# Output projection of attention as a phase of its own, with one level of Strassen, O through DRAM

## The chip, the cores and the metric

One core of a Trainium2 chip. The metric is the device time in microseconds (us) of one execution, the median of several runs. A core has five engines that matter here: PE (TensorE, matmul; its weight loads are listed as PEld), DVE (VectorE), ACT (ScalarE), POOL (GpSimd) and SP (SyncE), which issues nearly all of this kernel's transfers (DMA) from one queue, in order.

## The reference

```python
def _A_ref(x, k_cache, v_cache, wq, wo):
    ...
    Hq, Dh = 32, 128
    W = min(4096, max(256, Sk // 4))
    ...
    scores = jnp.einsum("bhqd,bhkd->bhqk", q, k) * (Dh ** -0.5)
    p = _softmax(scores, axis=-1)
    o = jnp.einsum("bhqk,bhkd->bhqd", p, v)
    return (lambda x, *d: x.transpose(*d))(o, 0, 2, 1, 3).reshape(B, Sq, Hq * Dh) @ wo
...
mod = (_silu(c) @ w_mod).reshape(c.shape[0], 6, 1, -1)
sa, ca, ga, sb, cb, gb = (mod[:, 0], mod[:, 1], mod[:, 2], mod[:, 3], mod[:, 4], mod[:, 5])
h = _layernorm(x, axis=-1) * (1 + ca) + sa
x = x + ga * _A_ref(h, A_k_cache, A_v_cache, A_wq, A_wo)
h = _layernorm(x, axis=-1) * (1 + cb) + sb
x = x + gb * _B_ref(h, B_w_gate, B_w_up, B_w_down)
```

x has 2048 rows of 576 channels; 32 query heads share 16 heads of keys and values, of which the last 512 rows count. `_B_ref` is a gated FFN with 4608 hidden channels. Everything is float32; a product is made as three matmuls of float32r operands that are split into a high and a low part (hi x lo, lo x hi, hi x hi).

## The kernel before

**Attention** works in blocks: one head and 512 rows of x, 4 tiles of 128 rows each. There are 128 blocks in an order `seq`, in two halves of 64 (rows 0 to 1023, then 1024 to 2047), and N = 512 steps n, one for each tile. A step of the main loop issues, for different blocks at once: a quarter of the query projection two blocks ahead (`qproj`, PSUM tile qp), the scores of tile n + 2 (`scores`, st), the transposes of tile n (`transp`, st again), the exponential of tile n + 2 (`expo`), one of four parts of P times V of the block before (`pv`, ot), and both halves of one tile of the output projection of the block before that (`wo_acc`, wo). `wo_acc` has three matmuls for each half of 288 columns; DVE then takes the result from PSUM, divides it by the sum of its softmax row (rs) and adds it to x, which stays in SBUF as four tiles xs[0] to xs[3]. Before that, ACT and DVE split O (tile ov) into its parts, and the rows of wo are loaded for each head, multiplied by the gate on POOL, and split on ACT and POOL (`load_o`, `scale_o`, `split_o`).

**Weights of the FFN** are prepared beside attention. The FFN itself uses one level of Strassen, and its operands' sums are formed and split by 135 jobs: 72 for gate and up ("ab"), after each eight of them one for the channels left over ("tail"), and 54 for down. A job is loaded at step n (`bg_load`), summed on POOL at n + 3, split on ACT and POOL at n + 6 and n + 7, and stored to DRAM at n + 8 and n + 9 (`bg_store`, tensors wsc and dsc). A new job starts every 3 steps. A job's room is used again three jobs later. An ab job has 3 loads and 3 stores, a tail job 4 loads and 24 stores, a down job 4 loads and mostly 3 stores. The rooms lie in those halves of x that are not in use: xs[2] and xs[3] in the first half, xs[0] and xs[1] in the second; around the change of halves no job runs.

**The order.** From step 8 on, the kernel's main instructions on each engine are held in the program's order (`keep_order`, `pin`); those that are not pinned may be moved by the scheduler of the tile framework. All these transfers leave from SP's one queue. A DMA that has to wait for a semaphore holds those behind it.

**FFN.** 72 rounds of seven products (PSUM tiles a, b, c) with sums of down projections between them (PSUM tile w, matmuls of 288 columns). Its operands come from scr (normalised x, in seven Strassen sums, formed in the second half of attention from xs[0] and xs[1]), wsc and dsc; the first of them are loaded while attention ends.

Of the kernel before, what the change touches and what calls it, by code (L numbers as in the profile page):

```python
# [13 lines left out]
OP = mybir.AluOpType  # L14
# [30 lines left out]
def adaln_block_kernel(ctx: ExitStack, tc: tile.TileContext, x, k_cache, v_cache, wq, wo, w_gate, w_up, w_down,  # L45
# [25 lines left out]
    actx = ExitStack()  # L71
    wp = actx.enter_context(tc.tile_pool(name="wp", bufs=1))
# [6 lines left out]
    def ps_sc():  # L79
        return psum("st", 3, [P, BLK])  # L80

    def ps_pt():
        return psum("st", 3, [P, BLK])
# [7 lines left out]
    def ps_wide():  # L91
        return psum("wo", 2, [P, BLK])
# [194 lines left out]
    at = actx.enter_context(tc.tile_pool(name="at", bufs=1))  # L287
# [8 lines left out]
    sbc = at.tile([P, NC + 1, P], F32, tag="ov", name="sbc", bufs=2)  # L296
    extra = at.tile([P, 4 * P], F32, tag="extra", name="extra")
    scale, shift, gate = mod_rows("scale", wp), mod_rows("shift", wp), mod_rows("gate", wp)
# [59 lines left out]
    load_mod(2, range(NC + 1))  # L358
# [6 lines left out]
    p2 = [ps_wo(), ps_wo()]  # L365
# [12 lines left out]
    p2 = [ps_wo(), ps_wo()]  # L378
# [20 lines left out]
    gate2 = [ps_wo(), ps_wo()]  # L399

    def gate_mm(ks):
        mod_mm(2, ks, gate2)
        if NC in ks:
            for j in range(2):
                nc.scalar.activation(gate[:, j * D2 : (j + 1) * D2], gate2[j], AF.Copy)

    def chunks1(ks):
        if 0 in ks:
            new_hT(1)
        for k in ks:  # L410
            p = ps_wide()
            for t in range(TPB):
                ln_channels(1, t, k, p)
            ln_shifted(1, k, p)


    RA, SA, RB, SB, KR, KS, VR, VS = {}, {}, {}, {}, {}, {}, {}, {}
    wm = {}
    QT, SUM, RS, PP, PT, OT, OP_, QP = {}, {}, {}, {}, {}, {}, {}, {}
# [74 lines left out]
    def expo(n):  # L494
# [21 lines left out]
    def pv(b, k):  # L516
# [7 lines left out]
        if k == KT - 1:  # L524
            o = at.tile([P, 2, BLK], F32R, tag="ov", name="ov", bufs=2)
            keep_order(nc.scalar.activation(o[:, 0, :], OP_[b], AF.Copy))
            nc.vector.tensor_sub(o[:, 1, :], OP_[b], f32(o[:, 0, :]))
            OT[b] = o
            del OP_[b], PT[b]

    def wo_acc(b, i, j):
        half, hd, blk = blk_of(b)
        cols = slice(i * P, (i + 1) * P)
# [33 lines left out]
    inst, inst_of = [], []  # L567
    for b, (half, hd, blk) in enumerate(seq):
        hh = half * H + hd
        for i in (len(inst) - 1, len(inst) - 2):  # L570
            if i >= 0 and inst[i][0] == hh:
                break
        else:
            i = len(inst)
            inst.append([hh, b, b])
        inst[i][2] = b
        inst_of.append(i)

    def load_o(i):
        RB[i] = load_b(wo, (inst[i][0] % H) * DH)  # L580

    def scale_o(hh):
        pin(nc.gpsimd.tensor_mul(RB[hh], RB[hh], gate))

    def split_o(hh):
        SB[hh] = split_b_hi(RB[hh])

    def split_o_lo(hh):
        split_b_lo(RB.pop(hh), SB[hh])

# [23 lines left out]
    at_n(-3, gate_mm, (0,))  # L614
# [8 lines left out]
    at_n(0, gate_mm, (1,))  # L623
    at_n(2, gate_mm, (2,))
    at_n(3, gate_mm, (3, 4))
# [10 lines left out]

    def o_first(i):
        return TPB * (inst[i][1] + 2)

    def o_free(i):  # L640
        return TPB * (inst[i][2] + 3)
# [12 lines left out]
    for hh in range(len(inst)):  # L654
        n = max(o_first(hh) - 7, o_free(hh - 2) if hh > 1 else 5)
        assert n < o_first(hh)
        at_n(n - 5, load_o, hh)
        at_n(max(n - 2, 4), scale_o, hh)
        at_n(n, split_o, hh)
        at_n(min(n + 1, o_first(hh) - 1), split_o_lo, hh)  # L660
    for b in range(2, NB):
        at_n(N // 2 - 34 + b, load_x, b)
# [18 lines left out]
    def pair_norm(pair, t, h, mul, add):  # L681
        for i in range(2):
            b = 2 * pair + i
            mv, y = LN[b][:2]
            pin(nc.vector.tensor_scalar(h[i], xs[b][:, t, :], mv[:, t, 0:1], y[:, t : t + 1],
                                        op0=OP.subtract, op1=OP.mult))
            mul.tensor_mul(h[i], h[i], rows2["scale"])
            add.tensor_add(h[i], h[i], rows2["shift"])

    def pair_sums(pair, t, h, ta, tb, ea, eb):  # L690
        lo, hi = slice(0, D2), slice(D2, D)
        ea.tensor_sub(ta[:, 0, :], h[1][:, lo], h[0][:, lo])
        ea.tensor_sub(ta[:, 1, :], h[1][:, hi], ta[:, 0, :])
        eb.tensor_sub(tb[:, 0, :], h[1][:, hi], h[1][:, lo])
        eb.tensor_sub(tb[:, 1, :], h[0][:, hi], ta[:, 1, :])
        d = scr[pair].rearrange("c p t d -> p c t d")
        for c0, src in ((0, h[0].rearrange("p (c d) -> p c d", c=2)), (2, ta), (4, h[1][:, None, hi]), (5, tb)):
            n = src.shape[1]
# [588 lines left out]
```

## Time and profile before

| | us |
|---|---|
| median of 3 runs | 3077.04 |
| lowest, highest | 3075.27, 3080.04 |
| span of the profiled execution | 3073.5 |
| wo matmuls of attention, first and last start | 66.2, 1824.3 |
| first product of the FFN | 1827.5 |

The page of the profile counts the busy time of each engine and groups the costliest instructions; the views used below are the busy time in stretches of the run, the instructions in order of time on one engine, and the instructions of one tile with their shortest, median and longest duration. The line L36 stands for every recorded operation, since a helper issues them all, so groups are told apart by their tiles: `x<-wo,rs,x` is the eviction of the output projection, `wo<-wb,ov` its matmul. SPq is the issue of a DMA by SP; its duration is that of the issue, not of the transfer.

### The profile page before, as it was taken

To read this page: it belongs to the slowest core of one execution; us is meant where nothing else is said; L and a number is where in the kernel's file an instruction comes from. 1 tells how busy PE (TensorE), PEld (TensorE's weight loads), DVE (VectorE), ACT (ScalarE), POOL (GpSimd) and SP (SyncE) were. 2 spreads that over 40 slices of the span, in tenths; PEclk is the share of its full clock that TensorE was granted. 3 is DMA by queue.
4 is the path that set the end of the run, shared out by engine and by line. 5 is a ranking of instruction groups with operands and counts; after the bars stand their busy time and mean duration, and the time that the engine had idled before them with its cause. 6 is when DMAs were issued, how large, how long until landed. Compare 5 with 4: busy or idle time off the path is not lost.

```text
span 3073.5 us, 49691 instructions
## 1 busy us (share of the span) xinstructions
PE 3043.3 (99%) x17029; PEld 2639.8 (86%) x17029; DVE 2144.9 (70%) x4180; ACT 1434.9 (47%) x2993; POOL 1550.0 (50%) x1777
## 2 busy tenths in 40 slices
PE   8999999999999999999999999999999999999998
PEld 6888888888888888888888888888888888888887
DVE  6777777777888877777777776555555665555557
ACT  5656656556555555555655553322232323322322
POOL 3656655655341646556565625545444453433443
PEclk9999999999999999999999999999999999999999
DMA  4565655655311245544444456767766676666664
GB/s 144 155 171 157 159 160 159 162 157 152 116 32 59 82 105 162 135 114 123 116 118 120 114 193 215 224 202 233 235 199 199 213 249 197 201 199 199 199 207 128
DMA packets 545308, 496.71 MB, mean 162 GB/s; under 512 B 161952, under 2 KB 424096, under 8 KB 544160
## 3 DMA queue, kind: packets, MB, share of 16 engines
q1 hardware_dynamic: 544448, 493.53, 55.9%
q8 instruction: 136, 2.23, 0.3%
q14 instruction: 116, 0.95, 0.1%
q10 hardware_dynamic: 608, 0.00, 0.0%
HBM read 355.67 MB, written 137.72 MB: 161 GB/s over the span
## 4 chain that ended last, share of the span: by engine, by line
PE 96%; DVE 2%; ACT 1%; DMA 1%; issue 0%; POOL 0%; SPq 0%; DVEq 0%; ACTq 0%
PE st L36 19%; PE a L36 15%; PE wo L36 14%; PE qp L36 13%; PE w L36 13%; PE ot L36 11%; PE c L36 7%; PE b L36 4%; DVE x L36 1%; ACT wm L36 0%; DMA ts<-scr 0%; ACT pp L36 0%; DMA wm<-in_w_mod_dram 0%; DVE ptt L36 0%; DVE hl L36 0%
## 5 line engine op out<-in xcount | busy, mean ns | idle before, releaser
L36 DVE TENSOR_TENSOR x<-w,x 128x288 f32<-128x288 f32 x980 | 442.6, 456 | 457.2 <-PE w L36 450.9
L36 PE MATMUL wo<-wb,ov 128*128 128x288 f32 x3072 | 615.6, 308 | 2.2 <-DVE ov L36 1.2
L36 ACT ACTIVATE ptt<-st 128x512 fp32r<-128x512 f32 x512 | 306.6, 599 | 634.7 <-PE st L36 634.7
L36 PEld LDWEIGHTS w<-sd,hl 128*128 128x128 f32 x3036 | 511.7, 188 | 90.0 <-DVE x L36 2.9
L36 PE MATMUL a<-hc,sw 128*128 128x512 f32 x2016 | 580.7, 393 | 3.7 <-DVE v L36 3.4
L36 PE MATMUL w<-sd,hl 128*128 128x288 f32 x3036 | 562.4, 294 | 3.7 <-ACT hl L36 1.4
L36 DVE SCALAR_TENSOR_TENSOR x<-wo,rs,x 128x288 f32<-128x288 f32 x1024 | 513.3, 512 | 60.0 <-PE wo L36 10.7
L36 DVE TENSOR_REDUCE neg<-st 128x1 f32<-128x512 f32 x512 | 352.5, 688 | 287.0 <-PE st L36 286.2
L36 PEld LDWEIGHTS wo<-wb,ov 128*128 128x128 f32 x3072 | 481.6, 189 | 49.3 <-DVE ov L36 1.8
L36 PE MATMUL ot<-ptt,vs 128*128 128x512 f32 x1536 | 443.2, 395 | 1.7 <-DVE ptt L36 1.6
L36 PE MATMUL qp<-hTm,wa 128*128 128x512 f32 x1536 | 442.8, 397 | 2.1 <-DVE hTm L36 1.9
L36 PE MATMUL st<-kt,qt 128*128 128x512 f32 x1536 | 436.3, 392 | 1.0 <-DVE ptt L36 1.0
L36 POOL TENSOR_TENSOR hl<-vs,hl 128x512 fp32r<-128x512 f32 x139 | 181.6, 1308 | 425.5 <-ACT hl L36 425.5
L36 PEld LDWEIGHTS a<-hc,sw 128*128 128x128 f32 x2016 | 354.6, 188 | 42.8 <-DVE v L36 4.5
L36 ACT ACTIVATE pp<-st,neg 128x512 f32<-128x512 f32 x512 | 350.8, 685 | 45.2 <-DVE neg L36 44.7
L36 DVE TENSOR_TENSOR ptt<-st,ptt 128x512 fp32r<-128x512 f32 x512 | 348.3, 680 | 5.1 <-ACT ptt L36 4.2
L36 POOL TENSOR_TENSOR x<-x,x 128x384 fp32r<-128x384 f32 (+6 forms) x305 | 246.0, 817 | 203.1 <-ACT x L36 177.7
L36 PEld LDWEIGHTS st<-kt,qt 128*128 128x128 f32 x1536 | 287.6, 188 | 65.3 <-DVE ptt L36 2.2
L36 PEld LDWEIGHTS st<-ident,pp 128*128 128x128 f32 x2048 | 254.1, 139 | 71.2 <-ACT pp L36 4.0
L36 PE MATMUL st<-ident,pp 128*128 128x128 f32 x2048 | 306.3, 272 | 3.0 <-ACT pp L36 2.1
L36 PE MATMUL c<-hc,sw 128*128 128x512 f32 x1008 | 301.8, 393 | 0.0
L36 PEld LDWEIGHTS qp<-hTm,wa 128*128 128x128 f32 x1536 | 260.8, 188 | 27.7 <-issue 2.3
(151 smaller groups left out, 3711.6 us busy)
## 6 DMA issues: line engine op xcount, KB each, us to landing
sw<-wsc SPq DMA_DIRECT2D x504, 320.0 KB
sd<-dsc SPq DMA_DIRECT2D x249, 288.0 KB
wsc<-x SPq DMA_DIRECT2D x72, 448.0 KB
raw<-in_A_wo_dram SPq DMA_DIRECT2D x66, 288.0 KB
dsc<-x SPq DMA_DIRECT2D x51, 336.0 KB
raw<-in_A_wq_dram SPq DMA_DIRECT2D x64, 256.0 KB
wsc<-x SPq DMA_DIRECT2D x72, 192.0 KB
wsc<-x SPq DMA_DIRECT2D x54, 256.0 KB
```

The source lines that it names most:

```text
L36: i = got(*args, **kw)
```

## The change

1. **Attention without `wo_acc`.** `pv`'s last part multiplies O by the reciprocal sums and leaves it in float32 (no split); O goes to DRAM (oscr). The sums lie along partitions in rs and are wanted along columns, so they go to DRAM (rscr) and come back as a tile rb of 128 equal rows. That makes three DMAs for each block: rscr from rs, rb from rscr, oscr from ov.
2. **The operands from wo** are formed by 48 jobs beside attention, one each 9 steps: four loads of 128 x 96, seven operations on POOL (multiply by the gate, four differences), one store of 896 x 96 to wosc.
3. **A new phase** follows attention: 32 visits, of 128 rows of four row blocks and eight heads each. A visit has the seven products of Strassen's method in the form with running sums (`STAGES`), of 12 matmuls each, and DVE adds each running sum from PSUM to x. The sums of O's pieces are formed on POOL (`v_sum`) and split on ACT and DVE (`v_split`), the weights split on ACT and POOL or DVE (`w_split`). The normalisation and the sums of xs[0] and xs[1] for the FFN move into its last visits, in place.
4. **Rooms and times.** x is no longer needed in SBUF during attention. All weight jobs use xs[0] and xs[1], one after the other from step 9, still every 3 steps; x is loaded again 40 steps before the end. The first loads of the FFN are issued in and after the last visit. PSUM: st has 4 buffers in place of 3, wo 1 in place of 2. The gate of attention is made like the other rows of the modulation, beside attention.

```diff
     def expo(n):
         if i == TPB - 1:
             nc.vector.reciprocal(RS[b], SUM[b])
+            at_late(n - 1, put_rs, b)
+            at_late(n + 2, get_rs, b)
+            at_late(n + 6, put_o, b)
     def pv(b, k):
         if k == KT - 1:
-            o = at.tile([P, 2, BLK], F32R, tag="ov", name="ov", bufs=2)
-            keep_order(nc.scalar.activation(o[:, 0, :], OP_[b], AF.Copy))
-            nc.vector.tensor_sub(o[:, 1, :], OP_[b], f32(o[:, 0, :]))
+            o = at.tile([P, BLK], F32, tag="ov", name="ov", bufs=2)
+            by_tile = RB.pop(b).rearrange("p (q i) -> p i q", i=TPB)
+            nc.vector.tensor_mul(o.rearrange("p (i q) -> p i q", i=TPB),
+                                 OP_[b].rearrange("p (i q) -> p i q", i=TPB), by_tile)
             OT[b] = o
-    def wo_acc(b, i, j):
-        p = down_mm(OT[b][:, 0, cols], OT[b][:, 1, cols], SB[inst_of[b]], j, ps_wo())
-        xv = xs[blk][:, i, j * D2 : (j + 1) * D2]
-        nc.vector.scalar_tensor_tensor(xv, p, RS[b][:, i : i + 1], xv, op0=OP.mult, op1=OP.add)
+    def put_rs(b):
+        keep_order(nc.sync.dma_start(rscr[b % 4], RS[b]))
+    def get_rs(b):
+        RB[b] = at.tile([P, BLK], F32, tag="rb", name="rb", bufs=2)
+        keep_order(nc.sync.dma_start(RB[b], rscr[b % 4].rearrange("p t -> (p t)").partition_broadcast(P)))
+    def put_o(b):
+        to = oscr[half][hd // 8][:, :, 2 * (blk % 2) + hd % 2, hd // 2 % 4, :]
+        keep_order(nc.sync.dma_start(to, OT.pop(b).rearrange("p (i q) -> p i q", i=TPB)))
...
-    slots = [(n, 0) for n in range(7, n1 - 43, STEP)] + [(n, 1) for n in range(n1 + 44, N - 14, STEP)]
+    slots = list(range(9, N - 50, STEP))[: len(jobs)]
...
+    def wo_load(k):
+        for half, (i, j) in enumerate(((0, 1), (5, 2))):
+            for h, slot in enumerate((i, j)):
+                pin(nc.sync.dma_start(t[:, slot, :], wo[r0 : r0 + P, n0 : n0 + DW]))
+    def wo_store(k):
+        pin(nc.sync.dma_start(wosc[g // 4][:, :, g % 4, c * DW : (c + 1) * DW], WOJ.pop(k)))
+    for k in range(3 * (H // 2)):
+        at_n(32 + 9 * k, wo_load, k)
+        at_n(36 + 9 * k, wo_sums, k)
+        at_n(40 + 9 * k, wo_store, k)
...
+    STAGES = ((0, 0, "a", 0, 0), (4, 3, "c", 1, 1), (5, 4, "a", 0, 1), (6, 2, "c", 0, 1),
+              (2, 5, "a", 1, 1), (1, 1, "b", 0, 0), (3, 6, "a", 1, 0))
...
+    for v in range(VISITS):
+        for s, (plane, combo, tag, row, col) in enumerate(STAGES):
+            for j in range(4):
+                for n, (l, r) in enumerate(three(o[:, 0, j, :], o[:, 1, j, :], w[:, 0, j, :], w[:, 1, j, :])):
+                    nc.tensor.matmul(p, l, r, start=fresh and j == 0 and n == 0, stop=j == 3 and n == 2,
+                                     skip_group_check=not fresh)
+            dst = xs[2 * pair + row][:, t, col * D2 : (col + 1) * D2]
+            nc.vector.tensor_add(dst, p, dst)
+            beside(v, s)
+    lctx.close()
+    for _ in range(9):
+        load_w(True)
```

How the instructions stand. First PE in the middle of attention, one step before and one after the change (st the scores and transposes, ot P times V, qp the query projection):

```order
L36 MATMUL st<-kt,qt 128x512 x3
L36 MATMUL st<-ident,pp 128x128 x4
L36 MATMUL wo<-wb,ov 128x288 x3
L36 MATMUL ot<-ptt,vs 128x512 x3
L36 MATMUL wo<-wb,ov 128x288 x3
L36 MATMUL qp<-hTm,wa 128x512 x4
```

```order
L36 MATMUL qp<-hTm,wa 128x512 x3
L36 MATMUL st<-kt,qt 128x512 x3
L36 MATMUL st<-ident,pp 128x128 x4
L36 MATMUL ot<-ptt,vs 128x512 x3
L36 MATMUL qp<-hTm,wa 128x512 x4
```

Two groups of three matmuls are gone from the step, and nothing stands in their place. Next DVE in attention after the change, in one block (neg the maxima of a tile's scores, ptt the low part of the transposed exponentials, ov the multiplication that waits for rb):

```order
L36 TENSOR_REDUCE neg<-st 128x1
L36 TENSOR_TENSOR ov<-ot,rb 128x512
L36 TENSOR_TENSOR ptt<-st,ptt 128x4x128
L36 RECIPROCAL rs<-sum 128x4
L36 TENSOR_REDUCE neg<-st 128x1
```

The evictions into x are gone; the one operation that needs a transfer, ov, stands between the maxima and the splits of later tiles. Last SP in attention after the change, in the first tail job (numbers of the buffers shown; wsc0 to wsc3 are the targets of the tail's stores, x0, x1 and extra their sources):

```order
L36 DMA wsc1_301<-x0_101 32x3x128
L36 DMA wsc1_301<-extra_109 32x4x128
L36 DMA woj_1762<-in_A_wo_dram 128x96 x4
L36 DMA oscr0_0_286<-ov_1707 512x1x128
L36 DMA rb_1791<-rscr1_283 128x512
L36 DMA wsc2_302<-x1_102 224x1x128
L36 DMA wsc2_302<-x0_101 32x3x128
```

The four loads of a wo job, the store of O and the load of rb stand between the tail's two groups of twelve stores, which before held nothing but a load of v.

More of the change, by code (lines that the diff above doesn't have):

```diff
@@ L653, in adaln_block_kernel @@
         at_n(n - 2 if gg else 1, make_v, gg)
[L654 to L660, printed above, removed]
     for b in range(2, NB):
-        at_n(N // 2 - 34 + b, load_x, b)
+        at_n(60 + b, load_x, b)
+    for b in range(2):
+        at_n(N - 40 + b, load_x, b)
     def norm_block(b, n_stats, n_apply, n_t, step, sc_, sh_, mul, add):
```

299 lines of the change are left out of this document (192 added, 107 removed).

## The prediction

> **What bounds the kernel now.** I read the head of the page first, then the busy time by stages, then the order of time on PE inside one attention step, and last the queue that issues the transfers. The page and two stretches of the run (columns: stretch and its length; busy us of PE, PEld, DVE, ACT, POOL with counts; granted clock; DMA share; GB/s):
>
> ```profile
> span 3073.5 us, 49691 instructions
> PE 3043.3 (99%) x17029; PEld 2639.8 (86%) x17029; DVE 2144.9 (70%) x4180; ACT 1434.9 (47%) x2993; POOL 1550.0 (50%) x1777
> 400.00:500.00 100.00, 100.00 (x575) 86.93 (x574) 75.85 (x140) 60.31 (x133) 58.66 (x77) 1.00 0.59 159
> 654.00:676.00 22.00, 22.00 (x128) 19.07 (x127) 16.44 (x32) 12.97 (x28) 14.24 (x20) 1.00 0.74 207
> ```
>
> PE never rests in attention, at full clock, and every other engine has a quarter of its time free. So a matmul taken away is worth its spacing, as long as nothing else fills up first. The spacing is read from the starts of one step (timeline of PE; the last row, from the view of the tile wo, has the first and last start of all of its matmuls):
>
> ```profile
> 1500.39 0.60 PE L36 MATMUL st<-ident,pp 128*128 128x128 f32 x4
> 1500.75 0.64 PE L36 MATMUL wo<-wb,ov 128*128 128x288 f32 x3
> 1501.22 0.86 PE L36 MATMUL ot<-ptt,vs 128*128 128x512 f32 x3
> 1501.92 0.56 PE L36 MATMUL wo<-wb,ov 128*128 128x288 f32 x3
> 1502.32 0.63 PE L36 MATMUL qp<-hTm,wa 128*128 128x512 f32 x2
> 1502.78 0.62 PE L36 MATMUL qp<-hTt,wa 128*128 128x512 f32 x2
> 1503.24 0.84 PE L36 MATMUL st<-kt,qt 128*128 128x512 f32 x3
> 1503.92 0.60 PE L36 MATMUL st<-ident,pp 128*128 128x128 f32 x4
> L36 PE MATMUL wo<-wb,ov x3072: 288/295/403, 66.2 to 1824.3; 128*128 128x288 f32 x192
> ```
>
> The first three wo matmuls hold PE from 1500.75 to 1501.22, 0.47 us, the second three 0.40 us: 0.87 us of a step. The first group's extra 0.07 us stands behind the transposes and will stand before whatever follows them. So the change frees 0.80 us per step. A whole step takes (1824.3 - 66.2)/512 = 3.43 us, so 2.63 us would be left.
>
> **What the change removes and adds on PE.** Removed: 512 steps x 0.80 = 410 us, and the early gate product, 20 matmuls:
>
> ```profile
> 27.16 1.14 PE L36 MATMUL wo<-wm,sbc 128*128 128x288 f32 x4
> ```
>
> at 1.14/4 = 0.285 us each, 6 us. Added: 32 visits x 7 stages x 12 = 2688 matmuls of 288 columns. FFN already runs this shape between others:
>
> ```profile
> 2300.09 0.56 PE L36 MATMUL w<-sd,hl 128*128 128x288 f32 x3
> 2300.49 0.85 PE L36 MATMUL a<-hc,sw 128*128 128x512 f32 x3
> ```
>
> 0.40 us for three, 0.133 us each: 2688 x 0.133 = 358 us. PE alone gives 3073.5 - 410 - 6 + 358 = 3016 us. That is the floor that Strassen pays for; whether it is reached depends on what the shorter step runs into.
>
> **DVE, ACT, POOL in the shorter step.** From 75.85 us per 100 DVE works 2.60 us a step; two evictions go, and one multiplication (ov from ot and rb) takes the place of a subtraction of the same shape:
>
> ```profile
> L36 DVE SCALAR_TENSOR_TENSOR x<-wo,rs,x 128x288 f32<-128x288 f32 x1024 | 513.3, 512 | 60.0 <-PE wo L36 10.7
> L36 DVE TENSOR_TENSOR x<-w,x 128x288 f32<-128x288 f32 x980 | 442.6, 456 | 457.2 <-PE w L36 450.9
> L36 DVE TENSOR_TENSOR v<-v,g 128x512 f32<-128x512 f32 x72 | 52.9, 735 | 7.6 <-DVE v L36 0.5
> ```
>
> 2.60 - 1.02 = 1.58 of 2.63 us. ACT has 2.07 us and loses a little, POOL has 2.01 us and swaps work of about the same size (the scaling and splitting of wo for the wo jobs' sums). Both stay under 80%. Here I add nothing.
>
> **The SP queue in the shorter step.** This is where I expect the end to be set. All loads and stores go out on SP, in order, and a DMA that waits holds back those behind it. The preparation of the FFN weights runs on a clock of steps: a job each 3 steps, each ninth a tail job with 24 stores. One tail and the three jobs behind it, in which SP catches up (timeline of SP: start, us, count at the end):
>
> ```profile
> 639.82 1.25 SPq L36 DMA_DIRECT2D wsc<-x  x2
> ...
> 653.65 0.43 SPq L36 DMA_DIRECT2D wsc<-extra  x1
> 655.16 0.40 SPq L36 DMA_DIRECT2D x<-in_B_w_gate_dram  x1
> 655.60 0.94 SPq L36 DMA_DIRECT2D x<-in_B_w_up_dram  x2
> 656.59 3.20 SPq L36 DMA_DIRECT2D wsc<-x  x3
> 661.98 0.37 SPq L36 DMA_DIRECT2D x<-in_B_w_gate_dram  x1
> 662.41 0.93 SPq L36 DMA_DIRECT2D x<-in_B_w_up_dram  x2
> 663.39 0.43 SPq L36 DMA_DIRECT2D raw<-in_A_k_cache_dram  x1
> 663.86 0.43 SPq L36 DMA_DIRECT2D raw<-in_A_wo_dram  x1
> 664.39 2.43 SPq L36 DMA_DIRECT2D wsc<-x  x3
> 666.87 2.96 SPq L36 DMA_DIRECT2D raw<-in_A_wq_dram  x3
> 669.94 0.53 SPq L36 DMA_DIRECT2D x<-in_B_w_gate_dram  x1
> 670.83 0.82 SPq L36 DMA_DIRECT2D x<-in_B_w_up_dram  x2
> 671.71 1.28 SPq L36 DMA_DIRECT2D wsc<-x  x2
> 673.08 0.99 SPq L36 DMA_DIRECT2D wsc<-extra  x1
> 674.12 0.68 SPq L36 DMA_DIRECT2D raw<-in_A_v_cache_dram  x1
> 675.80 0.37 SPq L36 DMA_DIRECT2D x<-in_B_w_gate_dram  x1
> ```
>
> The tail's stores hold SP from 639.82 to 654.08, 14.3 us. Then, with SP behind, a job takes (675.80 - 655.16)/3 = 6.88 us with its share of the q, k, v and wo loads; 16.4 of the 20.64 us are issue, 4.2 us (1.4 a job) are gaps and waits, the longest from 659.79 to 661.98, until a store has landed and its room can be loaded again. So a round of nine jobs (27 steps) needs 9 x 6.88 + 14.3 = 76.2 us of SP. Today the round has 27 x 3.43 = 92.6 us: SP is late only behind a tail, and makes it good. After the change PE wants the next round after 27 x 2.63 = 71.0 us. Even with nothing added SP is too slow.
>
> And it gets more. A round has 6.75 blocks with three DMAs each (rscr, rb, oscr), three wo jobs with four loads and a store, and loses 3.4 loads of wo: 20.25 + 15 - 3.4 = 32 DMAs. Their nearest rows (min/median/max ns):
>
> ```profile
> L36 SPq DMA_DIRECT2D wsc<-x x342: 332/566/2089, 82.7 to 1239.2; - x171
> L36 SPq DMA_DIRECT2D x<-in_B_w_down_dram x216: 328/424/1683, 1211.4 to 1756.4; - x108
> ```
>
> About 0.45 us and a gap of 0.05 us each: 16 us. Upper end: 76.2 + 16 = 92.2 us a round. Lower end: the added issues fill all the gaps of the nine jobs, 9 x 1.4 = 12.7 us: 79.5 us. I take 88, nearer the upper end: half of the added DMAs stand where SP doesn't wait, and 512 KB a block and 1.4 MB of wo a round have to be moved too, 4 MB net, which at the 207 GB/s of the second stretch is 20 us, more than their issue.
>
> Does PE feel it? Yes: rb stands in this queue. The multiplication by rb sits in DVE's order between the maxima (neg) and the splits (ptt) of the next tiles; while it waits, no exponential and no transpose follows. rb is asked for two steps, 5.3 us, before it is used, and in the tail 12 stores are ahead of it and 12 behind, ahead of the next one. Also the job's own sums on POOL and copies on ACT are held in the program's order. So SP's round becomes the round of all. The gate and up jobs are 81, nine rounds: 9 x (88 - 71.0) = 153 us lost; ends 9 x 8.5 = 76 and 9 x 21.2 = 191.
>
> [...]
>
> **The other places.** The 54 down jobs have no tails: seven DMAs, some 3.2 us of issue; four shared loads, 0.9 us; 3.9 added ones at 0.5, 2.0 us; and 1.4 us of waits make 7.5 of 7.9 us for three steps. Bounds 0 and 54 x 0.7 = 38 us (all waits doubled, half of it hidden); I take 15. In a visit of 7 x 12 x 0.133 = 11.2 us, DVE has 7 x (0.456 + 0.735) = 8.3 us and 0.6 us for the next weights' split (1152 columns at the 512's rate), 80%, and a bank is written again one stage (1.6 us) after its sum: bounds 0 and 2 us a visit (64); I take 15. For the start of FFN the row is
>
> ```profile
> L36 SPq DMA_DIRECT2D sw<-wsc x504: 319/356/1771, 1795.7 to 3033.1; - x168
> ```
>
> The first weights are asked for 32 us before the first product (1827.5). Now they, nine of 320 KB, stand behind the end of the visits, whose space they take: bounds 0 and 2.9 MB at 207 GB/s, 14 us; I take 8.
>
> **Sum.** 3016 + 153 + 15 + 15 + 8 = 3207 us in the profiled execution. The median of the three runs before is 3077.04, 3.5 us above its profiled execution's span: **3210 us**, slower by 4.3%.
>
> **The rivals.** (1) SP hides it: the added DMAs fill the gaps, rb is early enough, rounds run at PE's 71 us. Then 3016 and some 18 for the other places, with the 3.5, **3037 us**, faster by 1.3%. For it: the DMA share is 0.59, and SP catches up today. Against: 76.2 is over 71.0 before anything is added. (2) SP binds but the gaps are filled: 79.5 us a round, 3016 + 76 + 16 for the other places + 3.5 = **3111 us**, slower by 1.1%. (3) The stalls feed each other: a late rb delays the store of ov, for which SP then waits; a round takes 97 us, and the down jobs lose their 38: 3016 + 234 + 38 + 23 + 3.5 = **3314 us**. (4) The visits wait for DVE, 64 in place of 15: **3259 us**, on top of the forecast.
>
> **How the numbers follow.** Forecast 0.50, (1) 0.17, (2) 0.14, (3) 0.12, (4) 0.07. What this kernel's measurement can tell from no change is about 0.2%, 6 us. Faster comes from (1) and a little from (2), if the other places cost nothing and its rounds come out shorter still: 0.19; the same 0.04; slower 0.77. The forecast's own range goes from 3130 (rounds of 81 us) to 3250 (rounds of 92 us). Over all cases 8 in 10 lie from 3045 to 3290: that leaves out most of (1) and the worse half of (3).
>
> **What would show it.** Right: a step of 3.2 us or more up to about 850 us of the run, PE's idle time there put down to DVE (ov, ptt) or to ACT and behind these to DMA rb; SP issuing without rest; then 2.7 us steps, and visits of 11 to 12 us. Wrong: steps of 2.65 us with tails in between, which is rival (1); visits well over 12 us; or steps that stay long after the wo jobs have ended, which would mean that an engine and not the queue binds.

## The result, and the profile after

| | us |
|---|---|
| before, median of 4 runs (lowest to highest) | 3078.53 (3075.27 to 3080.04) |
| after, median of 4 runs (lowest to highest) | 3420.89 (3414.53 to 3421.84) |
| ratio, 95% interval | 1.1103 (1.1086 to 1.1119) |
| span of the profiled execution, before and after | 3073.5, 3418.4 |

The change makes the kernel 11% slower, 342 us. The forecast was 3210 us: the direction was right, the size was not, and the time lies outside the range. Medians below leave out one slow execution of e17, of 6689 us.

The page of the changed kernel begins so (its span, busy time by engine, and the first line on the chain that ended last):

```profile
span 3418.4 us, 50512 instructions
PE 3111.2 (91%) x16629; PEld 2644.1 (77%) x16629; DVE 2085.1 (61%) x3621; ACT 1497.4 (44%) x3067; POOL 1746.9 (51%) x2124
PE 54%; DMA 18%; SPq 8%; POOL 7%; DVE 5%; issue 5%; ACT 3%; POOLq 0%; ACTq 0%; DVEq 0%
```

Before, PE was busy for 99% of the span. Now a third of the chain is transfers, their issue and POOL. Four stretches of 100 us show where (columns as in the prediction's windows: busy us of PE, PEld, DVE, ACT, POOL with counts; granted clock; DMA share; GB/s):

```profile
400.00:500.00 100.00, 73.48 (x359) 58.73 (x357) 49.15 (x76) 48.67 (x109) 62.34 (x87) 0.86 0.72 181
1200.00:1300.00 100.00, 89.41 (x439) 71.13 (x438) 56.60 (x91) 56.68 (x134) 68.04 (x125) 0.98 0.79 186
1500.00:1600.00 100.00, 100.00 (x514) 82.15 (x513) 67.16 (x106) 59.44 (x131) 23.64 (x41) 1.00 0.42 100
1900.00:2000.00 100.00, 92.01 (x665) 90.16 (x664) 87.88 (x112) 41.02 (x62) 63.42 (x36) 0.98 0.34 119
```

The first lies in the gate, up and tail jobs, the second in the down jobs, the third behind all weight jobs, the last in the visits. Only the third looks like the kernel before: PE always busy at full clock, 514 matmuls. The first has 359: the step is 1.4 times as long, every engine is idle for much of it, and the clock is 0.86. In the visits it is DVE that is nearly full.

To compare stretches I use rounds of 27 steps, read from the starts of DVE's maxima (neg, one a step). From step 9 on, nine rounds with tails (the "ab part") take 97.1 us on the mean, six in the down part 85.0, the last two 72.4. One tail shows what happens in a round. SP's timeline (start, us, count at the end):

```profile
269.23 1.53 SPq L36 DMA_DIRECT2D wsc<-x  x2
...
274.91 1.20 SPq L36 DMA_DIRECT2D wsc<-x  x2
276.15 0.43 SPq L36 DMA_DIRECT2D wsc<-extra  x1
276.63 1.87 SPq L36 DMA_DIRECT2D woj<-in_A_wo_dram  x4
278.54 1.64 SPq L36 DMA_DIRECT2D raw<-in_A_wq_dram  x3
280.23 1.23 SPq L36 DMA_DIRECT2D wsc<-x  x2
...
286.70 0.45 SPq L36 DMA_DIRECT2D wsc<-extra  x1
288.09 0.40 SPq L36 DMA_DIRECT2D x<-in_B_w_gate_dram  x1
288.53 0.94 SPq L36 DMA_DIRECT2D x<-in_B_w_up_dram  x2
```

The tail's stores hold SP from 269.2 to 287.2. What waits for them, in the timelines of ACT, POOL and PE (in brackets the idle time just before and what ended it):

```profile
288.06 1.04 ACT L36 ACTIVATE x<-x 128x384 fp32r<-128x384 f32 x2 [14.71 <-DMA wsc<-x]
289.48 0.59 ACT L36 ACTIVATE ptt<-st 128x512 fp32r<-128x512 f32 x1
```

```profile
291.23 0.46 POOL L36 TENSOR_TENSOR extra<-x 128x128 f32<-128x128 f32 x1 [16.84 <-DMA x<-in_B_w_up_dram]
```

```profile
275.06 2.26 PE L36 MATMUL ot<-ptt,vs 128*128 128x512 f32 x9
290.36 1.65 PE L36 MATMUL qp<-hTm,wa 128*128 128x512 f32 x3 [13.04 <-DVE qt L36]
291.80 1.06 PE L36 MATMUL st<-ident,pp 128*128 128x128 f32 x4
292.51 2.06 PE L36 MATMUL qp<-hTm,wa 128*128 128x512 f32 x4
294.36 1.27 PE L36 MATMUL st<-kt,qt 128*128 128x512 f32 x3
295.47 0.60 PE L36 MATMUL st<-ident,pp 128*128 128x128 f32 x4
```

ACT has the high part of a job next in its order, and that job writes into the room from which the tail is still being stored; ACT stands for 14.7 us with the copies and exponentials of attention behind it, PE for 13.0. POOL waits for loads that SP could not issue until the tail was out. Then PE runs its first matmuls at half speed: three of 512 columns in 1.65 us, against 0.84 in the step shown before. Over the whole stretch from 75 to 900 us (the waits: who, for what, us in total, times, longest):

```profile
POOL extra L36 <- DMA x<-in_B_w_up_dram: 207.3, 22, 18.6
ACT x L36 <- DMA wsc<-x: 146.0, 26, 16.7
DVE ptt L36 <- ACT ptt L36: 140.5, 121, 15.4
PE st L36 <- ACT pp L36: 94.9, 15, 16.4
DVE ov L36 <- DMA rb<-rscr: 50.3, 35, 4.8
```

rb, in the last row, is not among the long ones: 50 us in all, and never more than 4.8. Last, the visits and the FFN: the first matmul of a visit starts at 1728.8, and the first product of the FFN is in the row of the tile hc (shortest, median, longest ns; first and last start):

```profile
L36 PE MATMUL a<-hc,sw x2016: 387/393/632, 2164.5 to 3405.9; 128*128 128x512 f32 x184
```

So attention ends 99 us earlier than before (1728.8 against 1827.5), the visits take 436 us, and the FFN 1254 us against 1246.

### The profile page after: what moved, and what is told of

Same layout as the page of the kernel before. It is cut to its first block, busy times and chain, and to the rows that moved or that the text cites. A ratio compares the mean times of both kernels' runs of the same rounds, so it can differ in the third digit from the quotient of the medians.

```text
span 3418.4 us, 50512 instructions
## 1 busy us (share of the span) xinstructions
PE 3111.2 (91%) x16629; PEld 2644.1 (77%) x16629; DVE 2085.1 (61%) x3621; ACT 1497.4 (44%) x3067; POOL 1746.9 (51%) x2124
## 3 DMA queue, kind: packets, MB, share of 16 engines
q1 hardware_dynamic: 720352, 619.86, 64.9%
## 4 chain that ended last, share of the span: by engine, by line
PE 54%; DMA 18%; SPq 8%; POOL 7%; DVE 5%; issue 5%; ACT 3%; POOLq 0%; ACTq 0%; DVEq 0%
PE a L36 17%; PE w L36 12%; PE c L36 9%; SPq L36 8%; PE st L36 6%; DMA wsc<-x 5%; PE b L36 4%; PE qp L36 4%; DMA dsc<-x 4%; POOL x L36 3%; PE ot L36 3%; DMA x<-in_B_w_up_dram 2%; DMA x<-in_B_w_down_dram 2%; DVE vh L36 2%; DMA rb<-rscr 1%
## 5 line engine op out<-in xcount | busy, mean ns | idle before, releaser
L36 PE MATMUL st<-kt,qt 128*128 128x512 f32 x1536 | 474.8, 414 | 129.9 <-ACT pp L36 125.6
L36 PE MATMUL qp<-hTm,wa 128*128 128x512 f32 x1536 | 457.5, 410 | 54.2 <-DVE qt L36 52.2
L36 PE MATMUL ot<-ptt,vs 128*128 128x512 f32 x1536 | 486.5, 429 | 12.1 <-DVE ptt L36 8.0
L36 PEld LDWEIGHTS qp<-hTm,wa 128*128 128x128 f32 x1536 | 288.8, 194 | 131.4 <-DVE qt L36 66.8
L36 PEld LDWEIGHTS st<-ident,pp 128*128 128x128 f32 x2048 | 262.7, 144 | 100.5 <-issue 21.7
L36 PE MATMUL st<-ident,pp 128*128 128x128 f32 x2048 | 318.9, 279 | 21.3 <-DVE rs L36 12.0
L36 PEld LDWEIGHTS ot<-ptt,vs 128*128 128x128 f32 x1536 | 266.9, 196 | 50.6 <-DVE ptt L36 13.0
L36 ACT ACTIVATE x<-x 128x384 fp32r<-128x384 f32 (+2 forms) x228 | 110.8, 522 | 293.4 <-DMA wsc<-x 158.6
L36 POOL TENSOR_TENSOR x<-x 128x128 f32<-128x128 f32 (+3 forms) x315 | 165.8, 540 | 84.6 <-DMA x<-in_B_w_up_dram 77.9
```

What stands on the lines that cost most here:

```text
L36: i = got(*args, **kw)
```

## The experiments

Times are medians; where only one run was made, none is given an interval. Runs of the kernel before beside them took 3078 to 3081 us. "ab" and "down" are mean rounds of the nine and six rounds named above.

### Floor and base

**e1: nearly no weight jobs.**

```diff
+    jobs = [j for j in jobs if j[1] == 0]
-    slots = list(range(9, N - 50, STEP))[: len(jobs)]
+    slots = [9, 12, 15, 200, 203, 206]
```

> 129 of the 135 weight jobs are left out; the FFN reads the weights of the six that remain over and over, so its time is the same. All theories that put the loss on the jobs (queue, rooms, bytes) expect attention at 2.67 us a step, as in the stretch of the changed kernel from 1500 to 1700 us: 512 x 2.67 = 1367 us in place of 1662, visits and FFN unchanged, in all 3418 - 295 = about 3123 us. If the three new DMAs of each block (rscr, rb, oscr) stall the steps by themselves, steps stay at 2.8 us or more: 3190 us or more. My forecast's floor, with visits of 11.2 us, would be 3016 + 15.

Measured: 3139 us; ab 75.0, down 72.7, visits begin at 1449.0. In the middle of attention:

```profile
800.00:900.00 100.00, 100.00 (x516) 82.19 (x514) 67.67 (x106) 59.36 (x131) 22.48 (x40) 1.00 0.42 105
```

Nearly all of the 280 us between this kernel and the changed one lie in the jobs' part of attention (the visits take 439 us here). And the floor is above the kernel before: even with the weights' preparation taken away for nothing, the change loses 60 us.

**e8: the kernel before under the short step.**

```diff
-        if ok(b - 2):
-            wo_acc(b - 2, i, 0)
...
-        if ok(b - 2):
-            wo_acc(b - 2, i, 1)
```

> The kernel before with the output projection's matmuls and evictions left out of the step (wo is still loaded, scaled and split): its own jobs and queue under the short step, nothing added. My prediction's 76.2 us a round: nine rounds of 76 in place of 72.4, the rest at 2.68 us a step, attention 512 x 2.68 + 9 x 4 = 1408 us in place of 1758: 3079 - 350 = about 2730 us. If the jobs' rooms and waits make rounds of 85 to 90 us even so: 2830 us or more.

Measured: 2726 us, seven rounds with jobs of 76.9 us. This is the prediction's base, 76.2 us, almost to the point. But in e1, with hardly a job, the same seven rounds take 75.3 us: under the short step the queue of before binds by 1 or 2 us, not by the 5 that the prediction had.

### One thing out of the queue

**e5: no tail stores. e6: no wo jobs up to step 356. e7: no rscr and rb. e10: O's store for 16 of 128 blocks.**

```diff
-            for q in (0, 1) if part == 0 else (2, 3):
+            for q in () if f else (0, 1) if part == 0 else (2, 3):
```

```diff
-    for k in range(3 * (H // 2)):
-        at_n(32 + 9 * k, wo_load, k)
+    for k in range(12):
+        at_n(356 + 9 * k, wo_load, k)
```

```diff
-            at_late(n - 1, put_rs, b)
-            at_late(n + 2, get_rs, b)
```

```diff
-            at_late(n + 6, put_o, b)
+            if blk_of(b)[0] == 0 and blk_of(b)[1] < 8:
+                at_late(n + 6, put_o, b)
```

> The 24 stores of each tail job but the first are left out (the FFN reads the weights of the first jobs over and over, its time is the same). If a round's time is the sum of what SP issues, the eight later rounds lose 24 x 0.55 = 13 us or more, from 97 to about 84: 3418 - 8 x 13 = about 3314 us. If waits for landed transfers bind and the tail only moves them, rounds stay over 92 us: 3370 or more.

> 36 of the 48 wo jobs are left out and the other twelve run in the last slots (steps 356 to 463), so up to step 356 there are none; the visits read the same rows of wo again. Issue theory: 15 DMAs a round x 0.55 = 8 us less in nine rounds, some 4 x 6 in the down part, 3418 - 96 = about 3320. If their POOL operations (seven, some 3 us a job) hold the jobs' sums too, more: 3300. If the room waits bind: rounds over 93, 3380 or more.

> The two DMAs that turn the sums into rb are left out for each block; ov is multiplied by ones, so the division by the softmax sums is left out; the third DMA, O's store, stays. Issue theory: 13.5 DMAs a round x 0.55 = 7 us less in nine rounds, some 5 in six: 3418 - 95 = about 3325. If rb is how the queue's lateness gets into the steps, as my prediction had it, PE no longer feels the queue but through the jobs' own operations, and rounds fall below 85: 3290 or less. If it gets in through POOL and ACT alone and the issues matter little: 3390 or more.

> O's store is left out for 112 of the 128 blocks; the visits read the same rows of O over and over. Issue price alone: 6.75 a round x 0.55 us x 13 rounds = 48 us, 3372 us. If SP's waits for ov (99 us in all) count too: 3420 - 48 - 60 = about 3310 us. If bytes count (256 KB a block): between.

| | us | ab | down |
|---|---|---|---|
| changed kernel | 3421 | 97.1 | 85.0 |
| e5 without tail stores | 3316 | 86.3 | 82.5 |
| e6 without wo jobs | 3326 | 89.5 | 80.4 |
| e7 without rscr and rb | 3270 | 86.3 | 76.8 |
| e10 without O's store | 3338 | 92.7 | 79.0 |

Everything taken out of the queue shortens the round by at least the half microsecond a DMA that I had put in: 24 tail stores 12 us in the eight rounds that have lost them (0.5 each), 15 DMAs of wo jobs 7.6 us (0.5 each), 13.5 DMAs for rb 10.8 us (0.8 each), five stores of O a round (45 in nine rounds) 4.4 us (0.9 each). Nothing was hidden, in the ab part or in the down part. These prices hold the bytes of the DMAs and what waits for them too, and each comes from one run.

What SP does in a round, from its timeline between steps 36 and 198 (six rounds; issue is the sum of its DMAs' durations, short gaps are those up to 0.3 us, waits the longer ones):

| | DMAs | issue | short gaps | waits | round |
|---|---|---|---|---|---|
| before | 94.2 | 50.8 | 4.1 | 39.2 | 94.4 |
| e8 before without wo | 94.0 | 52.9 | 4.8 | 18.9 | 77.0 |
| changed kernel | 124.2 | 74.8 | 7.2 | 16.9 | 99.3 |
| e7 without rscr and rb | 111.7 | 66.4 | 6.2 | 15.5 | 88.2 |
| e5 without tail stores | 105.0 | 65.0 | 6.4 | 17.4 | 88.8 |

From e8 to the changed kernel 30.2 DMAs are added (the prediction had 32); SP's issue and short gaps grow by 24.3 us, and its waits hardly shrink. The 48 stores of the jobs alone take 31.5 us to issue in place of 29.2. The new issues, in the rows of their tiles:

```profile
L36 SPq DMA_DIRECT2D rb<-rscr x128: 319/625/1813, 41.3 to 1723.6; - x128
L36 SPq DMA_DIRECT2D oscr<-ov x128: 518/565/1360, 65.6 to 1728.6; - x128
L36 SPq DMA_DIRECT2D woj<-in_A_wo_dram x192: 328/442/2802, 136.3 to 1567.3; - x192
L36 SPq DMA_DIRECT2D wosc<-woj x48: 518/519/1479, 166.6 to 1587.5; - x48
```

### How it gets into the steps

**e9: rb's two DMAs without their ties** (the first stores ones, nobody reads the second's tile). **e13: as e9, one row of rb in place of 128.** **e2: half the bytes of the stores.**

```diff
-        keep_order(nc.sync.dma_start(rscr[b % 4], RS[b]))
+        keep_order(nc.sync.dma_start(rscr[b % 4], rs1))
...
-            by_tile = RB.pop(b).rearrange("p (q i) -> p i q", i=TPB)
+            by_tile = RB1[0].rearrange("p (q i) -> p i q", i=TPB)
```

```diff
-        keep_order(nc.sync.dma_start(RB[b], rscr[b % 4].rearrange("p t -> (p t)").partition_broadcast(P)))
+        keep_order(nc.sync.dma_start(RB[b][:1], rscr[b % 4].rearrange("p t -> (p t)").partition_broadcast(1)))
```

```diff
+            np_ = P if f == 0 else 64
-            pin(nc.sync.dma_start(to[0][:, :n], hi[:, :n]))
+            pin(nc.sync.dma_start(to[0][:np_, :n], hi[:np_, :n]))
```

> The two DMAs for rb stand in the queue as in the changed kernel, with the same bytes, but the first stores a tile of ones, so SP waits for no sums, and the second fills a tile that nobody reads, so DVE waits for no transfer; the division by the softmax sums is left out. Taking both DMAs away gave 3270. If their price is their issue (0.5 us each, 13.5 a round, 15 rounds), it comes back: 3270 + 100 = 3370 us. If the price is the tie between SP and DVE (SP waits for the sums of the step that the jobs hold up, DVE for rb), it stays away: 3300 or less.

> As e9, but the second DMA fills one row of 2 KB in place of 128: the same number of issues in the same places, 256 KB less a block (1.7 MB less a round); the division by the softmax sums is left out. With both DMAs gone the rounds up to step 198 took 88 us, with both at full size 98. If the slots in SP's queue are the price (a DMA's issue of some 0.55 us, whatever its size), 95 us or more a round and about 3375 us or more. If the bytes are the price, 90 or less and 3310 us or less.

> Every store of the gate, up and down jobs but those of the first job of each kind writes 64 of its 128 partitions: the same number of DMAs in the same places, 459 KB less for a gate/up job and 344 KB less for a down job. If bytes bind (the DMA engines), a round loses 8 x 0.459 MB at 190 GB/s = 19 us, from 100 to about 81, and the down jobs 1.3 us each: 3418 - 171 - 70 = about 3175 us. If the number of issues on SP binds, an issue costs nearly the same: 3390 us or more. If waits for landed stores bind (rooms that are used again three jobs later), something between: some 3300.

e9 took 3398 us. With the two DMAs gone it was 3270, with them there 3421: 128 of the 151 us are the DMAs themselves, and only 23 the waits of DVE for rb and of SP for the sums. So the path through rb that the prediction put first carries little. In the trace of the tail above the queue reaches PE through the jobs' own copies on ACT and sums on POOL; no run takes that tie away. e13 took 3320 us: the rounds between steps 36 and 198 are 98.1 us (e9), 93.2 (e13) and 88.2 (e7), so about half of rb's price is its 1.7 MB a round and half the two slots. Over the whole run the bytes are the larger part, 78 of the 128 us. (One row is also one piece to write in place of 128, so bytes and pieces go together here.)

e2 took 3354 us, ab 92.8, 67 us less than the changed kernel, and far from what bytes alone would have given. But it tests them badly. From 300 to 500 us, the changed kernel first, then e2:

```profile
300.00:500.00 200.00, 152.14 (x715) 121.27 (x715) 97.52 (x153) 101.30 (x230) 119.70 (x177) 0.87 0.74 190
```

```profile
300.00:500.00 200.00, 152.92 (x715) 122.37 (x714) 99.37 (x155) 105.40 (x238) 123.14 (x188) 0.86 0.68 161
```

The bytes a second fall by 15%, the DMA engines' share by 8% only. So a byte takes 8% more of the engines' time than in the changed kernel (0.68 at 161 GB/s against 0.74 at 190); why, no run here shows.

### Rooms and queues

**e3: a second set of rooms** in xs[2], xs[3] up to step 195. **e11: each block's three DMAs issued by ACT. e14: both.**

```diff
+        if slots[k] < 196:
+            b0 = 2 * (k % 2)
-        raw = bg_view(b0, (k % 3) * 4 * P, [4, w])
+        raw = bg_view(b0, (j % 3) * 4 * P, [4, w])
...
-        hi = bg_view(b0 + 1, (k % 2) * 7 * P, [8 if kind == "down" else 7, w])
+        hi = bg_view(b0 + 1, (j % 2) * 7 * P, [8 if kind == "down" else 7, w])
```

```diff
-        keep_order(nc.sync.dma_start(rscr[b % 4], RS[b]))
+        keep_order(nc.scalar.dma_start(rscr[b % 4], RS[b]))
...
-        keep_order(nc.sync.dma_start(to, OT.pop(b).rearrange("p (i q) -> p i q", i=TPB)))
+        keep_order(nc.scalar.dma_start(to, OT.pop(b).rearrange("p (i q) -> p i q", i=TPB)))
```

(j is k // 2 up to step 195.)

> The jobs up to step 195 (63 of 135, seven rounds) alternate between the rooms in xs[0], xs[1] and those in xs[2], xs[3], which lie idle there, so that a room is used again after six jobs (loads) or four (sums, high parts) in place of three and two; x is loaded into xs[2] and xs[3] later. The same DMAs and bytes. If the waits until a store has landed bind (SP before a load, ACT before the high part), the seven rounds fall from 100 to 76 to 80 us: 3420 - 7 x 22 = about 3265 us. If the number of issues or the bytes bind: within 30 us of 3420.

> The three DMAs of each block are issued by ACT in place of SP, in the same places of the program: the same DMAs and bytes. If SP's queue is what binds, rounds fall to what the jobs and the wo jobs need there, 76.9 + 7.6 = 84 us, and the down part to about 75: 3420 - 9 x 13 - 6 x 9 = about 3250 us, plus what ACT loses for the issues (20 a round x 0.5 = 10 us of its 15 free in a round: up to 40 us). If bytes or the path through rb bind, whoever issues: over 3370.

> The two edits that did little alone, together: each block's three DMAs on ACT's queue (rounds 98 in place of 99, SP waits 30 us a round) and the second set of rooms (89 us, SP's issues and short gaps 83). If there are two limits, SP's issues (83 us a round, 67 with the DMAs on ACT) and the waits until a room's store has landed (16 to 30, 6 with the second rooms), both fall at once only here: 67 + 6 = 73 us, so PE's 73 to 80 us in the first seven rounds, and with the down part as in e11 about 3420 - 7 x 20 - 10 = 3270 us. If rooms are the only limit: 89 as in e3, about 3330. If bytes are (19 MB a round at 215 GB/s): 88 or more, 3330 too.

| | us | issue | short gaps | waits | round, steps 36 to 198 |
|---|---|---|---|---|---|
| changed kernel | 3421 | 74.8 | 7.2 | 16.9 | 99.3 |
| e3 rooms | 3350, ratio 1.0879 (1.0862 to 1.0895) | 75.6 | 7.4 | 6.2 | 89.1 |
| e11 ACT's queue | 3390 | 61.6 | 5.3 | 31.2 | 98.2 |
| e14 both | 3352 | 64.9 | 5.5 | 19.3 | 89.6 |

More rooms take away 11 us of SP's waits and 10 us of the round: the wait until a room's store has landed is a real part. ACT's queue takes 15 us of issue and short gaps from SP, and SP's waits grow by 14: SP's issue time as such does not set the round. And together they give no more than the rooms alone. My account of two limits in series, which expected 73 to 80 us here, falls. Nor is it what is left in e14: issue and short gaps are 70 of 90 us. What e3 and e14 have in common is the traffic (e3 first, then e14):

```profile
300.00:500.00 200.00, 169.45 (x819) 135.78 (x818) 107.68 (x171) 117.83 (x266) 129.84 (x203) 0.92 0.85 219
```

```profile
300.00:500.00 200.00, 174.16 (x836) 139.03 (x834) 110.27 (x173) 120.36 (x272) 127.98 (x203) 0.94 0.83 220
```

219 and 220 GB/s at a DMA share of 0.83 to 0.85, against 190 at 0.74 in the changed kernel. The same view from step 36 to step 198, six rounds, gives the bytes of a round as rate times length (e8, the changed kernel, e14, and e15 of the next section):

```profile
142.78:604.83 462.05, 445.24 (x2238) 359.52 (x2237) 281.63 (x459) 337.12 (x756) 333.27 (x436) 0.99 0.72 196
141.91:737.94 596.03, 473.62 (x2241) 375.92 (x2240) 306.20 (x512) 308.81 (x700) 337.52 (x528) 0.90 0.77 196
144.44:682.30 537.86, 467.34 (x2246) 371.10 (x2244) 296.19 (x463) 313.66 (x706) 327.93 (x523) 0.95 0.83 216
147.43:643.04 495.61, 457.49 (x2246) 366.31 (x2244) 390.32 (x747) 315.94 (x706) 347.98 (x525) 0.96 0.82 213
```

e8 moves 15.1 MB a round and the changed kernel 19.5, both at 196 GB/s: the round has grown just as its bytes have. With the second rooms the rate is higher, and it is nearly the same in four kernels whose rounds and DMAs on SP differ: 215 GB/s in e3 (89.1 us, 125 DMAs), 216 in e14 (89.6, 105), 213 in e15 (82.6, 112), 216 in e16 (81.5, 103). So the rate of the transfers accounts for these rounds better than the number of issues on SP. It is not shown to be the limit: e15 and e16 have fewer DMAs and other work on DVE beside 1.7 MB less, and e13, where only rb's 1.7 MB went, gained 5 us a round, where 196 GB/s would give 9. e11 speaks for the rate too: 15 us of issue and short gaps leave SP and 1 us the round, and from 300 to 500 us it moves 194 GB/s at a DMA share of 0.73, against the changed kernel's 190 at 0.74.

### Whole versions

**e12: P is divided by its sum on DVE before the transposes; rscr and rb are gone. e15: e12 and second rooms in both halves. e16: e15, O's store on ACT's queue, and two of the four loads of a wo or down job made one.**

```diff
-            at_late(n - 1, put_rs, b)
-            at_late(n + 2, get_rs, b)
...
+        nc.vector.reciprocal(RS[b][:, i : i + 1], SUM[b][:, i : i + 1])
+        nc.vector.tensor_scalar(PP[n], PP[n], RS[b][:, i : i + 1], None, op0=OP.mult)
...
-            nc.vector.tensor_mul(o.rearrange("p (i q) -> p i q", i=TPB),
-                                 OP_[b].rearrange("p (i q) -> p i q", i=TPB), by_tile)
+            nc.vector.tensor_copy(o, OP_[b])
```

```diff
         at_n(N - 40 + b, load_x, b)
+        at_n(N - 38 + b, load_x, b + 2)
```

```diff
+                src = wo[2 * g * P : 2 * (g + 1) * P, n0 : n0 + DW].rearrange("(h p) n -> p h n", h=2)
+                pin(nc.sync.dma_start(t[:, 0:2, :], src))
...
-        keep_order(nc.sync.dma_start(to, OT.pop(b).rearrange("p (i q) -> p i q", i=TPB)))
+        keep_order(nc.scalar.dma_start(to, OT.pop(b).rearrange("p (i q) -> p i q", i=TPB)))
```

> No rscr and no rb: DVE divides each tile of exponentials by its sum in place, before the transposes, and copies O out of PSUM; the result is the reference's. SP is freed as in the run without rb (3270 us); DVE gets 0.45 to 0.7 us a step and loses 0.1, from 67 to some 85 of 100. If DVE has that room: 3270 to 3290 us. If it doesn't (an operation in SBUF beside POOL takes up to twice as long, as vh did), steps of 2.9 us in the jobs' part: 3330 us.

> The exponentials divided in place (no rscr, no rb) and the second set of rooms, used also in the second half of attention (x is loaded a second time before the visits); the result is the reference's. Two limits: SP 66 + 6 of issue and 6 of waits, 78 us a round in the ab part, 75 in the down part: 3293 - 9 x 10 - 6 x 2 = about 3190 us. If one limit alone counted: over 3260. Neither theory brings it under the 3080 of the kernel before, since six jobs alone (e1) already took 3139.

> As e15, and O's store goes out on ACT's queue, and two of the four loads of each wo and down job become one: 6.75 + 3 DMAs a round less on SP in the ab part, 6.75 + 12 less in the down part. Two limits: the ab part at 75 us a round, the down part at 73.5: 30 us under e15, about 3160. If ACT's queue costs what SP gains: as e15.

| | us | ratio to before, 95% | ab | down |
|---|---|---|---|---|
| e12 | 3293 | 1.0693 (1.0675 to 1.0711) | 87.7 | 77.6 |
| e15 | 3266 | 1.0606 (1.0590 to 1.0622) | 85.0 | 77.5 |
| e16 | 3229 | 1.0482 (1.0465 to 1.0500) | 83.5 | 75.0 |

e12 keeps most of what e7 gained, and its 512 divisions are cheap (the row of pp on DVE):

```profile
L36 DVE TENSOR_SCALAR pp<-pp,rs x512: 464/490/2555, 32.8 to 1590.6; 128x512 f32<-128x512 f32 x171
```

e15 and e16 gained less than expected (3190 and 3160): with rounds of 82 us between steps 36 and 198 they stop at the rate at which e3 and e14 stop, 213 to 216 GB/s.

### The visits

**e4: the sums of O's pieces left out of the visits. e17: the same sums on DVE in place of POOL. e18: e17's edit on e16.**

```diff
-            v_sum(v + 1, s)
...
-        src = VRAW[v][:, plane] if plane < 4 else VSUM[v, (0, 2, 3)[plane - 4]]
+        src = VRAW[v][:, plane % 4]
```

```diff
-            nc.gpsimd.tensor_add(VSUM[v, 0], raw[:, 2], raw[:, 3])
+            nc.vector.tensor_add(VSUM[v, 0], raw[:, 2], raw[:, 3])
```

> The four sums of O's pieces on POOL are left out of each visit; the pieces themselves are split in their place. In the changed kernel the low part vh takes 0.68 us with POOL at rest and 1.2 to 1.4 beside a POOL operation. If that contention makes the visits long, every vh without a weight split beside it takes 0.68 us and the visits with weight splits fall from 14-15 us to 12-13: 30 us less, 3390 us. If the splits of the weights alone do it, or the normalisation in the last visits: under 8 us less.

> The four sums of O's pieces in each visit are formed by DVE in place of POOL; the same operations, the result is the reference's. DVE gets 4 x 0.69 = 2.8 us more a visit, but runs beside POOL only where weights are split or rows are normalised. If what lengthens the visits is DVE's operations in SBUF being slowed beside POOL, DVE works 7 x (0.45 + 0.68) + 2.8 = 10.7 of 11.2 us: visits without weight splits stay at 11.3, those with them fall from 14-15 to 12-13, 20 us less in all, about 3400. If it is the amount of DVE's work, visits grow to 13 us and more: 3440 us.

> The same edit on top of e16 (3229 us): 20 us less, about 3210, by the one account; 3250 by the other. Still over the kernel before.

A visit takes 128 rows of each of two of x's four row blocks. DVE in one visit of the changed kernel (its timeline; vh is a low part, x an eviction of a product from PSUM):

```profile
1903.48 0.69 DVE L36 TENSOR_TENSOR vh<-vt,vh 128x512 fp32r<-128x512 f32 x1 [0.25 <-ACT vh L36]
1904.37 0.46 DVE L36 TENSOR_TENSOR x<-c,x 128x288 f32<-128x288 f32 x1 [0.20 <-PE c L36]
1905.03 1.78 DVE L36 TENSOR_TENSOR vh<-vr,vh 128x512 fp32r<-128x512 f32 x1 [0.21 <-ACT vh L36]
1906.74 0.45 DVE L36 TENSOR_TENSOR x<-a,x 128x288 f32<-128x288 f32 x1
1907.11 1.41 DVE L36 TENSOR_TENSOR vh<-vr,vh 128x512 fp32r<-128x512 f32 x1
```

From 1905.0 to 1911.4 POOL forms the sums. A low part then takes 1.4 to 1.8 us in place of 0.69, while the evictions stay at 0.45. The rows of vh in the changed kernel, and in e17:

```profile
L36 DVE TENSOR_TENSOR vh<-vr,vh x128: 672/1051/2798, 1709.7 to 2158.0; 128x512 fp32r<-128x512 f32 x128
L36 DVE TENSOR_TENSOR vh<-vt,vh x96: 674/692/2604, 1712.8 to 2153.1; 128x512 fp32r<-128x512 f32 x96
```

```profile
L36 DVE TENSOR_TENSOR vh<-vr,vh x128: 675/684/2757, 1705.5 to 2128.8; 128x512 fp32r<-128x512 f32 x128
L36 DVE TENSOR_TENSOR vh<-vt,vh x96: 674/685/3029, 1708.7 to 2122.8; 128x512 fp32r<-128x512 f32 x96
```

e4: 3375 us, ratio 1.0954 (1.0935 to 1.0972), visits 400 us from their first matmul to the FFN's first product. e17: 3396 us, ratio 1.1037 (1.1018 to 1.1057), visits 421 us, 15 less than the changed kernel though DVE has four operations more in each. That is the slowing beside POOL, shown with the work unchanged. It is only a part of what the visits cost: they take 436 us, 78 over PE's 32 x 11.2, of which leaving out the sums altogether (e4) gains 36. e18: 3208 us, ratio 1.0419 (1.0402 to 1.0437), the shortest whole version with the change, and still slower than the kernel before. Visits without a weight split mostly take 11.2 to 11.6 us, as forecast; those with one 14 to 15 in the changed kernel, and the three that also carry the normalisation of x 17 to 25, 29 us over 3 x 11.2 together; no run takes the normalisation out.

## Why the prediction was wrong, step by step

The forecast's steps against the measured ones, in the time of the profiled execution (rounds: e1 gives the part without jobs):

| step | forecast | measured |
|---|---|---|
| attention without stalls, to the first visit | 1827.5 - 416 = 1411 | 1449 (e1) |
| stall in nine rounds with tails | 153 | 874 - 675 = 199 |
| stall in the down part | 15 | 510 - 436 = 74 |
| stall behind it | 0 | 7 |
| visits | 358 + 15 | 436 |
| FFN, longer by | 8 | 8 |

- **PE's floor was nearly right.** Matmuls removed and added cost what the rows said: visits of 11.2 us where nothing else binds. The step is 72.4/27 = 2.68 us, not 2.63, some 25 us over attention; the other 13 of the 38 were not traced to a cause.
- **The base of the queue had the right number, in part by luck:** 76.2 us a round, 77.0 in e8. But SP issues for 58 of these (with short gaps) and waits 19, where the prediction had 63.5 and 12.7, and with hardly a job (e1) the nine rounds take 75.0 us, not 71.0. The count of added DMAs was right: 32, 30 in the trace.
- **The step that failed is the price of what is added:** "About 0.45 us and a gap of 0.05 us each: 16 us", of which I took 12, since "half of the added DMAs stand where SP doesn't wait". Measured: SP's issue and short gaps grow by 74.8 + 7.2 - 52.9 - 4.8 = 24.3 us, 0.80 for each of 30.2 DMAs, and its waits fall by 2.0 us only, so the round is 22 us longer, not 12, and over my upper end (92.2). Nothing was hidden. And the bytes, whose "20 us" I had worked out, stood in the sum only as a reason to go near the upper end: at e13's price (5 us for 1.7 MB) the 4.4 MB added would be some 12 of the 22 us, an estimate from one run. How the 22 us divide between bytes and places in the queue stays open; that they are not SP's issue time alone is shown by e11. Rival 3 had the size of the ab part, 97 us, but by another mechanism: SP does not wait much more.
- **The same error made the down part:** a job costs SP (62.6 + 6.7)/9 = 7.7 us of issue and short gaps and 1.7 us of waits there (its timeline between steps 252 and 414), where I had 6.1 and 1.4. The round says 9.4 us a job (85.0/9), not 7.5, against the 7.9 that PE wants.
- **The path was the wrong one of the two named.** rb's ties cost 23 us in all (e9). By the trace, the weight jobs, held in order on ACT and POOL, bring the stall into the step (ACT stood 146 us and POOL 207 us for their DMAs up to 900 us). I named them in one sentence and built nothing on it.
- **The visits were mis-sized:** DVE at "7 x (0.456 + 0.735)" holds only while POOL rests (a low part took 0.68 us then, a median of 1.4 beside POOL), and the normalisation in the last visits stood in the sum at nothing. Measured are 436 us in place of 373: POOL's sums beside DVE are 15 us of it (e17). By the lengths of the visits, the three with the normalisation are 29 us over PE's time, and most of the rest lies in those with a weight split, which no run takes apart. Rival 4 named the place, DVE; its 64 us fell short of the 78 that came.
- **The start of the FFN:** the FFN takes 8 us more, as forecast, but that is luck: the 85th of its matmuls in the row of hc starts 52.7 us after the first (49.7 before), so the start costs 3 us, and the rest came later.
- **The clock.** The sum takes PE at full clock throughout. Behind the 13 us of rest before 290.4 PE worked at half speed for nearly 5 us (a granted clock of 0.50 from 290 to 295), and the granted clock of stretches of 100 us was 0.86 to 0.93 in the ab part. Its share of the 199 us can't be told apart here.

What stays open is which of bytes and the jobs' order on POOL holds a round at 82 to 90 us once the rooms are doubled; the near equal rates speak for the bytes.

## What to carry to other kernels

Where transfers already set the pace, price every one that is added in full, its bytes too (here 0.5 to 0.9 us each, by e5, e6, e7 and e10), and not at the median issue of the calm stretch. Don't let issue and bytes hide behind each other in the sum without a reason, and look for the waits that more work in front will not fill, such as a load into a room whose store has just been issued (e3's second rooms took away 11 of SP's 16.9 us of waits a round). When a change shortens the step, everything that runs on a clock of steps gets faster too: ask what its latency was hidden by. And before a phase is priced, ask which two engines work on SBUF side by side in it, since a duration read from the profile was measured in some company: here the same subtraction took 0.68 us with POOL at rest and 1.4 us beside it.

## What the runs showed of the hardware

- DVE's subtraction of two SBUF operands (128 x 512) took 0.68 us with POOL at rest and a median of 1.4 us where POOL worked beside it nearly throughout (94 of the visits' operations); its additions with one operand in PSUM stayed at 0.45.
- Three DMAs a block moved from SP to ACT (e11) left the round nearly as it was (99.3 and 98.2 us), with SP idle 14 us longer.
- A multiplication of 128 x 512 from PSUM and a tile read with a stride (ov from ot and rb) took 1.07 us, where a subtraction of that shape without one (ptt) took 0.69; no run took the stride away.
- After 12 to 13 us of rest (two places of the changed kernel, before 290.4 and 475.0 us) PE's matmuls of 512 columns followed each other at 0.43 us in place of 0.23, for 4 to 5 us.
